# VectorE scales whole-precision heads' probabilities; products of constants beside nine heads; weight words raised to a least value; last rows in one block

## The chip, the cores and the metric

The kernel runs on one NeuronCore of a Trainium2 chip. The core has five engines that each work through a list of their own, in order: TensorE (PE; its weight loads are shown apart as PEld), VectorE (DVE), ScalarE (ACT), GpSimd (POOL) and SyncE (SP), which here only issues DMAs. TensorE writes its results to PSUM, which has eight banks; the others work in SBUF and, except GpSimd, in PSUM. The metric is the device time of one execution in microseconds (us), lower is better.

## The reference

Attention with a memory term over 8 batches and 8 heads, 576 rows of 64 each, and behind it a feed-forward network over all 4608 rows:

```python
def _attn_ref(q, k, v, M_prev, z_prev, beta):          # q, k, v: 8 x 8 x 576 x 64
    scores = scale * np.matmul(q, k.transpose(0, 1, 3, 2))
    scores = np.where(causal, -1e9, scores)
    a = np.exp(scores - scores.max(-1, keepdims=True))
    a /= a.sum(-1, keepdims=True) + 1e-09
    local = np.matmul(a, v)
    q_p = phi(q)                                        # elu(q) + 1
    mem_out = (q_p @ M_prev) / (q_p @ z_prev + 1e-6)
    g = 1 / (1 + np.exp(-beta))                         # one per head
    return g * mem_out + (1 - g) * local

def _moe_ref(x, w_in, w_out):                           # x: 4608 x 512, w_in: 512 x 2048
    h = x @ w_in
    return (h * (1 / (1 + np.exp(-h)))) @ w_out         # 4608 x 512
```

q, k, v and M_prev are float32; w_in and w_out come as float64, so the kernel gets them as pairs of 32-bit words.

## The kernel before

**Three streams.** `attention()` works on the 64 heads (batch, head) one after the other. In iteration n it advances `scores` of head n and `values` of head n-1 by turns, one `yield` of each at a step, ten steps to a head. `preparation()` turns the 32 chunks (128 x 512 words) of the weights into the form that the matmuls take; `ffn()` works on 18 units of 256 rows. The loop at the end of the function mixes them: about three chunks of weights to a head, and units from the moment on at which the eight heads of the first batch are done (`done[0] >= H`). This gives a program order; the scheduler of the framework makes from it a fixed list for each engine, which the engine then follows strictly in order, waiting at the head of the list for what an instruction needs.

**Scores of a head.** L221 transposes q and k (DVE). Then come rows in blocks of 128: for block i the matmul L250 writes 128 x 128(i+1) scores to a PSUM bank of `ps_s`, L252 (DVE) adds the mask and takes the minimum of the negated scores, L254 (ACT) takes the exponential and its sum. 576 is four and a half blocks. The last 64 rows are done as two halves of their columns, 256 and 320, one on partitions 0 to 63 and one on 64 to 127 of one tile: two matmuls (L271 for whole heads, L274 for the others), two reductions L284, and `halves_of` (L289 to L291), which joins the two halves' minima and later their sums by three small DVE instructions each time. L299 and L302 make one factor for each row from the sums and the gate, and five L304 (POOL) scale the five blocks of probabilities.

**Whole heads and split heads.** The first `N_WHOLE = 10` heads are "whole": their matmuls take float32 operands as they are, and each such matmul shows as two TensorE instructions. The other 54 heads split each operand into a rounded part and a rest (float32r), and each matmul is one instruction.

**Values of a head.** L351 transposes the memory term's rows, L376, L393 and L384 transpose the scaled probabilities (L393 and L384 those of the last rows, two halves at a time), ACT copies them (L401), L414 and L422 multiply them with M_prev and v, and L425 copies the result out.

**Weights.** For each chunk ACT scales the low words (L150), DVE shifts and joins the high words (L152, L154), POOL adds the low part (L156), ACT takes the magnitude of the high words (L158), DVE multiplies the result with "magnitude at least LEAST" (L159), ACT rounds (L161) and POOL takes the rest (L162).

**Feed-forward.** L552 makes h (128 x 256, in the one bank of `ps_h`), L563 to L569 make silu, L532 adds to the two accumulators `acc`, each one bank of `ps_a`.

## Time and profile before

| | |
|---|---|
| median of 3 runs | 1315.68 us (1314.75 to 1318.42) |
| the profiled execution's own time | 1315.66 us |
| its span, first to last instruction | 1313.9 us |
| busy: PE, PEld, DVE, ACT, POOL | 96%, 83%, 68%, 67%, 63% of the span |
| mean granted TensorE clock | 0.975 |

The profile has three parts, each with another limit. Up to about 175 us only whole heads and weight preparation run; from there to about 1110 us feed-forward units run beside the heads; then feed-forward units run alone. The page gives busy shares over the whole span, so a stage is read from the view by windows, and the order of events on an engine from its timeline. In a timeline row the columns are start and duration in us, engine, line, operation, output and inputs, the tile sizes (for a matmul: stationary, then moving), the number of merged instructions and, in brackets, the idle time ahead and what ended it. The granted clock is known only from the first change of it that the profiler recorded; earlier windows show 1.00.

### The profile page before, as it was taken

What the parts mean: (1) busy time and instruction counts of PE and PEld (TensorE: products, weight loads), DVE (VectorE), ACT (ScalarE), POOL (GpSimd) and SP (SyncE); (2) the same over time, 40 slices, a digit from 0 to 9 for tenths busy, and PEclk for the clock granted to TensorE, in tenths of its full rate; (3) what the DMA queues carried; (4) which work ended last, traced back from release to release, by engine and by line L of the source; (5) the groups of instructions that cost most, each with busy time, mean ns of one, the idle gap of its engine ahead of it and who ended that gap; (6) DMA issues with size and microseconds to landing.
All of it is one profiled execution on the core that took longest, in us unless ns stands there. A gap on an engine that the chain in (4) does not pass through costs nothing.

```text
span 1313.9 us, 24653 instructions
## 1 busy us (share of the span) xinstructions
PE 1266.3 (96%) x7858; PEld 1084.0 (83%) x7858; DVE 898.1 (68%) x2472; ACT 884.5 (67%) x2143; POOL 822.9 (63%) x1133
## 2 busy tenths in 40 slices
PE   6988999999999999999999999999999999999998
PEld 2343458888999989998988989899898998999997
DVE  7988875778777777787767777777877775332222
ACT  6777866777787777777777777787878774322222
POOL 6878995777777777777777777767767763000000
PEclk9987779999999999999999999999999999999999
DMA  6766555555455555555555555555545432444444
GB/s 165 188 184 168 162 134 164 144 131 146 125 145 147 138 153 138 150 131 149 137 137 143 145 138 154 137 137 136 158 129 156 123 123 81 145 154 149 152 156 143
DMA packets 302994, 190.39 MB, mean 145 GB/s; under 512 B 258832, under 2 KB 267024, under 8 KB 302864
## 3 DMA queue, kind: packets, MB, share of 16 engines
q1 hardware_dynamic: 302864, 188.82, 51.9%
q8 instruction: 62, 1.02, 0.3%
q14 instruction: 68, 0.56, 0.1%
HBM read 173.02 MB, written 15.73 MB: 144 GB/s over the span
## 4 chain that ended last, share of the span: by engine, by line
PE 73%; DVE 11%; ACT 6%; issue 3%; POOL 3%; DMA 3%; SPq 1%; POOLq 0%; DVEq 0%; ACTq 0%
PE h L552 28%; PE acc L532 25%; PE x L422 7%; PE s L250 5%; PE tp L376 4%; PE tq L351 1%; PE x L414 1%; DVE s L252 1%; DVE wy L159 1%; DVE pl L407 1%; DVE st L290 1%; ACT p L254 1%; POOL p L304 1%; PE s L274 1%; DVE wy L154 1%
## 5 line engine op out<-in xcount | busy, mean ns | idle before, releaser
L552 PE MATMUL h<-xu,wi 128*128 128x256 f32 x2592 | 376.8, 287 | 8.7 <-DVE th L564 6.1
L552 PEld LDWEIGHTS h<-xu,wi 128*128 128x128 f32 x2592 | 343.0, 191 | 24.6 <-DVE th L564 7.8
L532 PE MATMUL acc<-wo,g 128*128 128x512 f32 x864 | 243.0, 398 | 0.0
L532 PE MATMUL acc<-flow,g 128*128 128x512 f32 x864 | 231.0, 394 | 0.5 <-DMA flow<-wo_s 0.5
L304 POOL TENSOR_SCALAR p<-p,st 128x384 f32<-128x384 f32 (+3 forms) x320 | 182.8, 592 | 75.3 <-DVE st L302 72.2
L564 DVE SCALAR_TENSOR_TENSOR th<-th,h 128x512 f32<-128x512 f32 x144 | 98.2, 683 | 143.5 <-ACT th L563 141.7
L532 PEld LDWEIGHTS acc<-flow,g 128*128 128x128 f32 x864 | 158.8, 188 | 33.6 <-DMA flow<-wo_s 1.0
L254 ACT ACTIVATE p<-s,st 128x128 f32<-128x128 f32 (+3 forms) x256 | 134.9, 528 | 69.9 <-DVE st L252 52.8
L569 POOL TENSOR_TENSOR g<-th,g 128x512 fp32r<-128x512 f32 x108 | 140.2, 1298 | 48.7 <-ACT g L567 46.9
L532 PEld LDWEIGHTS acc<-wo,g 128*128 128x128 f32 x864 | 149.1, 189 | 18.9 <-POOL p L304 0.5
L563 ACT ACTIVATE th<-h 128x512 f32<-128x512 f32 x144 | 85.9, 597 | 99.7 <-PE h L552 97.4
L407 DVE TENSOR_TENSOR pl<-tp,ph 128x384 fp32r<-128x384 f32 x216 | 118.5, 551 | 34.6 <-ACT ph L406 31.3
L252 DVE CUSTOM_DVE_ANT_0 s<-s,mask 128x128 f32<-128x128 f32 (+3 forms) x256 | 125.3, 491 | 23.1 <-PE s L250 19.6
L567 ACT CAST g<-th 128x512 fp32r<-128x512 f32 x144 | 89.2, 620 | 53.0 <-DVE th L564 52.1
L376 PE MATMUL tp<-ident,p 128*128 128x128 f32 x640 | 121.8, 291 | 3.2 <-POOL p L304 2.5
L552 PE MATMUL h<-xu,flow 128*128 128x256 f32 x864 | 122.6, 283 | 0.0
L406 ACT CAST ph<-tp 128x384 fp32r<-128x384 f32 x216 | 104.7, 490 | 26.1 <-PE x L422 21.2
L552 PEld LDWEIGHTS h<-xu,flow 128*128 128x128 f32 x864 | 112.8, 191 | 1.9 <-issue 0.3
L376 PEld LDWEIGHTS tp<-ident,p 128*128 128x128 f32 x640 | 82.2, 148 | 28.6 <-POOL p L304 9.0
L422 PE MATMUL x<-pl,vs 128*128 128x256 f32 x324 | 82.1, 308 | 0.9 <-DVE pl L407 0.9
L232 POOL TENSOR_TENSOR kk<-tt,kk 64x576 fp32r<-64x576 f32 x54 | 77.4, 1432 | 5.0 <-ACT kk L230 1.2
L422 PE MATMUL x<-ph,vs 128*128 128x320 f32 (+4 forms) x378 | 78.2, 275 | 1.4 <-POOL vs L316 0.8
(104 smaller groups left out, 2409.5 us busy)
## 6 DMA issues: line engine op xcount, KB each, us to landing
flow<-wo_s SPq DMA_DIRECT2D x144, 512.0 KB, 3.6
flow<-wi_s SPq DMA_DIRECT2D x72, 512.0 KB, 3.8
raw<-in_k SPq DMA_DIRECT2D x128, 72.0 KB, 2.5
raw<-in_q SPq DMA_DIRECT2D x128, 72.0 KB, 2.7
out<-o SPq DMA_DIRECT2D x36, 256.0 KB, 4.2
wraw<-in_moe_w_in SPq DMA_DIRECT2D x16, 512.0 KB, 4.4
qn<-in_q SPq DMA_DIRECT2D x64, 128.0 KB, 2.9
vr<-in_v SPq DMA_DIRECT2D x64, 128.0 KB, 2.5
```

The lines of the kernel that those rows point to most:

```text
L252: anchor["dve"] = nc.vector.tensor_tensor_reduce(s, s, mask[:, 3 * P - P * i:], QS, 3.0e38, ALU.add, ALU.min, st[:, i:i + 1]).ins
L254: nc.scalar.activation(pt, s, AF.Exp, bias=st[:, i:i + 1], scale=-1.0, accum_out=st[:, 10 + i:11 + i])
L304: nc.gpsimd.tensor_scalar(pb[x], pb[x], st[:, 15 + x:16 + x], 1.0, op0=ALU.mult, op1=ALU.mult)
L376: nc.tensor.transpose(t[:, o:o + P], pb[i][:, P * j:P * j + P], ident)
L406: nc.scalar.copy(ph[:, 0:o], t[:, 0:o])
L407: nc.vector.tensor_tensor(out=pl[:, 0:cut], in0=t[:, 0:cut], in1=f(ph[:, 0:cut]), op=ALU.subtract)
L422: nc.tensor.matmul(x[0:rows, q0:n], vs[0:n_k, j], part[0:n_k, o:o + n - q0], start=False, stop=last)
L532: nc.tensor.matmul(acc[t], ta, tb, start=p == 0 and c == 0 and n == 0, stop=p == NP - 1 and c == 1 and n == len(terms) - 1)
L552: nc.tensor.matmul(h[:, c], ta, tb, start=kk == 0 and n == 0, stop=kk == KD - 1 and n == len(terms) - 1)
L564: nc.vector.scalar_tensor_tensor(out=th, in0=th, scalar=1.0, in1=h, op0=ALU.add, op1=ALU.mult)
L567: nc.scalar.copy(hi, th)
L569: late.tensor_tensor(out=lo, in0=th, in1=f(hi), op=ALU.subtract)
```

## The change

1. *Scaling.* For whole heads the five scalings of the probabilities go from GpSimd to VectorE. For the other heads they stay.
2. *Last rows in one block.* For whole heads the last 64 rows are one block on 64 partitions: two matmuls of 288 columns into the two banks of one `ps_a` tile `sw`, one reduction over 64 x 2 x 288, one exponential, and one small copy in place of the six small instructions. The probabilities go to a tile `pw` (64 x 576), which takes the one buffer of the tag `vs`; in `values` they are transposed block by block, five transposes in place of three.
3. *Accumulators.* `ps_a` has one buffer of two banks in place of two buffers of one bank; the two accumulators of a unit are the halves of one tile.
4. *Products of constants.* `keep_busy` issues two 128 x 128 float32 matmuls (stationary: the identity; moving: 128 columns of the mask that are zero) at each step of iterations 0 to 8, each ordered behind the attention's latest matmul. They write a tile `idle` in the bank of `ps_h`, which nothing reads. There are 176 of them.
5. *Weights.* The magnitude of the high words is taken first and raised to LEAST (now 2^-15, without the factor 1.125) by a VectorE instruction with one input, ahead of the shift; the last multiplication goes away. There are still three VectorE instructions to a chunk; two of them now have one input (before, one).

```diff
+WARM = 2
...
-    LEAST = 2.0 ** -15 * 1.125
+    LEAST = 2.0 ** -15
...
-    ps_a = ctx.enter_context(tc.tile_pool(name="ps_a", bufs=2, space=PSUM))
+    ps_a = ctx.enter_context(tc.tile_pool(name="ps_a", bufs=1, space=PSUM))
...
+            nc.scalar.activation(w, f(high), AF.Abs)
+            nc.vector.tensor_scalar(w, w, LEAST, None, op0=ALU.max)
             nc.vector.tensor_scalar(
-                y, high, 3, 0x3FFFFFF8, op0=ALU.logical_shift_left, op1=ALU.bitwise_and)
+                y, y, 3, 0x3FFFFFF8, op0=ALU.logical_shift_left, op1=ALU.bitwise_and)
             nc.vector.scalar_tensor_tensor(
                 out=y, in0=high, scalar=0xC0000000, in1=y, op0=ALU.bitwise_and, op1=ALU.bitwise_or)
             nc.gpsimd.tensor_tensor(out=y, in0=y, in1=low, op=ALU.add)
-            nc.scalar.activation(f(high), f(high), AF.Abs)
-            nc.vector.scalar_tensor_tensor(
-                out=w, in0=f(high), scalar=LEAST, in1=w, op0=ALU.is_ge, op1=ALU.mult)
...
+        if whole:
+            n2 = S // 2
+            pt = pool.tile([P, S], F32, tag="vs", name="pw", bufs=NB["vs"])
+            banks = ps_a.tile([P, T // P, DM], F32, tag="a", name="sw")
+            for x in range(2):
+                nc.tensor.matmul(
+                    banks[up, x, 0:n2], qq[0:64, S - LAST:S], tt[0:64, n2 * x:n2 * x + n2], start=True, stop=True)
+            yield
...
+            anchor["dve"] = nc.vector.tensor_tensor_reduce(
+                s, s, seen, QS, 3.0e38, ALU.add, ALU.min, st[up, i:i + 1]).ins
+            nc.scalar.activation(
+                pt[up].rearrange("p (a b) -> p a b", a=2), s, AF.Exp, bias=st[up, i:i + 1], scale=-1.0,
+                accum_out=st[up, 10 + i:11 + i])
+            pb.append(pt)
+            yield
+            nc.vector.tensor_copy(st[down, 10 + i:11 + i], st[up, 10 + i:11 + i])
...
         for x in range(NQ):
-            nc.gpsimd.tensor_scalar(
-                pb[x], pb[x], st[:, 15 + x:16 + x], 1.0, op0=ALU.mult, op1=ALU.mult)
+            rows = up if whole and x == i else slice(0, P)
+            (nc.vector if whole else nc.gpsimd).tensor_scalar(
+                pb[x][rows], pb[x][rows], st[rows, 15 + x:16 + x], 1.0, op0=ALU.mult, op1=ALU.mult)
...
+                    if whole:
+                        for j, x0, q0 in spans:
+                            at, n_k = x0 + n - q0, min(P, S - P * j)
+                            nc.tensor.transpose(
+                                t[0:n_k, at - LAST:at], last[0:LAST, P * j:P * j + n_k], ident[0:LAST, 0:LAST])
...
+    def keep_busy(behind):
+        for _ in range(WARM):
+            with tc.issue_after(behind):
+                nc.tensor.matmul(idle[:, 0:P], ident, mask[:, 0:P], start=True, stop=True)
...
+    idle = ps_h.tile([P, 2 * T], F32, tag="h", name="idle")
...
+                behind = anchor.get("pe")
                 for _ in range(FIRST_STEPS):
                     one = one and next(first, "end") != "end"
...
+                if behind and n <= H:
+                    keep_busy(behind)
...
-            bank, tag = (ps_s, "s") if done[0] == B * H and u % 2 else (ps_a, "a")
-            acc = [bank.tile([P, DM], F32, tag=tag, name="acc") for _ in range(T // P)]
+            if done[0] == B * H and u % 2:
+                acc = [ps_s.tile([P, DM], F32, tag="s", name="acc") for _ in range(T // P)]
+            else:
+                banks = ps_a.tile([P, T // P, DM], F32, tag="a", name="acc")
+                acc = [banks[:, t] for t in range(T // P)]
```

The scheduler makes new lists from this. TensorE's list before, at the boundary between two whole heads (the last products of one head's values, `x`, and the first transposes of the next one's probabilities, `tp` from the tiles p_963 to p_1041):

```order
L422 MATMUL x<-ph,vr 64x64
L351 MATMUL tq<-ident,e 128x128 x2
L351 MATMUL tq<-ident,e 64x128
L250 MATMUL s<-tt,qf 128x512
L422 MATMUL x<-ph,vr 64x320
L271 MATMUL s<-tt,qf 64x256
L271 MATMUL s<-tt,qf 64x320
L376 MATMUL tp<-ident,p_963 128x128
L414 MATMUL x<-qp,mr 64x256
L376 MATMUL tp<-ident,p_988 128x128 x2
```

The same place in the changed list (`idle` is the output of the products of constants, `sw` the last rows' scores; lines are those of the changed file):

```order
L461 MATMUL idle<-mask,ident 128x128 x2
L370 MATMUL tq<-ident,e 128x128 x2
L370 MATMUL tq<-ident,e 64x128
L270 MATMUL sw<-tt,qf 64x288 x2
L251 MATMUL s<-tt,qf 128x128
L251 MATMUL s<-tt,qf 128x256
L446 MATMUL x<-ph,vr 64x320
L461 MATMUL idle<-mask,ident 128x128 x8
L395 MATMUL tp<-ident,p_867 128x128
L395 MATMUL tp<-ident,p_881 128x128 x2
L461 MATMUL idle<-mask,ident 128x128 x4
```

Twelve of a head's twenty products stand at this boundary, around the first transposes of the next head; the other eight stand in pairs between its products with v. VectorE's changed list around the scaling of one whole head (`p_515` to `p_572` and `pw` are the five blocks of probabilities, `wy` a chunk of weights):

```order
L284 COPY st<-st 64x1
L317 SCALAR_TENSOR_TENSOR st<-st,over 128x5
L320 RECIPROCAL st<-st 128x5
L155 TENSOR_SCALAR wy<-wy 128x512
L323 TENSOR_SCALAR p_515<-p_515,st 128x128
L323 TENSOR_SCALAR p_540<-p_540,st 128x256
L323 TENSOR_SCALAR p_556<-p_556,st 128x384
L323 TENSOR_SCALAR p_572<-p_572,st 128x512
L323 TENSOR_SCALAR pw<-pw,st 64x576
L156 TENSOR_SCALAR wy<-wy 128x512
```

The five scalings now stand in VectorE's list directly behind the factors, with weight work ahead and behind; before, they stood in GpSimd's list. In TensorE's list the feed-forward matmuls of the first unit, of which a few (nine of 24) stood among heads 2 to 8, now all stand behind the last product of constants; from the tenth head on the number of feed-forward matmuls ahead of each head differs from before by some tens at most, and 1236 of them stand behind the last transpose in both lists.

More of the change, by code (lines that the diff above doesn't have):

```diff
@@ L261, in scores @@
         i = NQ - 1
-        pt = pool.tile([P, 3 * P], F32, tag=f"p{i}", name=f"p{i}", bufs=P_BUFS)
-        halves = []
-        for side, other, x0, x1, o in ((slice(0, LAST), slice(LAST, P), 0, SPLIT, P),
-                                       (slice(LAST, P), slice(0, LAST), SPLIT, S, 0)):
-            s = ps_s.tile([P, 512], F32, tag="s", name="s")
-            s = s[:, 0:x1 - x0]
-            row = pair[side, o:o + x1 - x0]
-            more = mask[side, 0:x1 - x0] if x1 < S else mask[side, 4 * P + x0 - x1:]
-            if whole:
-                nc.tensor.matmul(s[side], qq[0:64, S - LAST:S], tt[0:64, x0:x1], start=True, stop=True)
-            else:
+        up, down = slice(0, LAST), slice(LAST, P)
+        if whole:
[6 more added lines that the diff above has]
+            yield
+            s = banks[up, :, 0:n2]
+            seen = mask[up, 0:n2]
+            seen = bass.AP(seen.tensor, seen.offset, [list(seen.ap[0]), [3 * P + LAST - n2, 2], [1, n2]])
+            anchor["dve"] = nc.vector.tensor_tensor_reduce(
[7 more added lines that the diff above has]
+        else:
+            pt = pool.tile([P, 3 * P], F32, tag=f"p{i}", name=f"p{i}", bufs=P_BUFS)
+            halves = []
+            for side, other, x0, x1, o in ((slice(0, LAST), slice(LAST, P), 0, SPLIT, P),
+                                           (slice(LAST, P), slice(0, LAST), SPLIT, S, 0)):
+                s = ps_s.tile([P, 512], F32, tag="s", name="s")
+                s = s[:, 0:x1 - x0]
+                row = pair[side, o:o + x1 - x0]
                 q0 = S - LAST if side.start == 0 else S
@@ L421, in values @@
                         n_k = LAST if whole and j == NQ - 1 else P
-                        nc.tensor.matmul(
-                            x[0:rows, q0:n], vs[0:n_k, j], part[0:n_k, o:o + n - q0], start=False, stop=last)
+                        anchor["pe"] = nc.tensor.matmul(
+                            x[0:rows, q0:n], vs[0:n_k, j], part[0:n_k, o:o + n - q0], start=False, stop=last).ins
             if whole:
```

37 lines of the change are left out of this document (18 added, 19 removed).

## The prediction

> **What bounds the kernel now.** I read the windows first, since the page's busy shares are means over stages with different limits. Columns: stretch, its length, then busy us and instructions of PE, PEld, DVE, ACT and POOL, granted clock, DMA share, GB/s.
>
> ```profile
> PEclk9987779999999999999999999999999999999999
> 0.00:17.50 17.50, 6.12 (x11) 2.39 (x11) 10.08 (x33) 7.49 (x17) 12.23 (x32) 1.00 0.61 133
> 17.50:66.80 49.30, 46.26 (x100) 18.64 (x100) 44.24 (x107) 37.17 (x90) 40.49 (x37) 1.00 0.72 191
> 66.80:175.00 108.20, 93.54 (x288) 43.67 (x286) 95.52 (x213) 83.23 (x199) 94.66 (x85) 0.73 0.60 163
> 300.00:1110.00 810.00, 798.42 (x5422) 734.34 (x5422) 605.00 (x1786) 612.03 (x1516) 585.75 (x861) 1.00 0.51 139
> 1110.00:1313.90 203.90, 198.63 (x1265) 179.50 (x1263) 57.39 (x96) 56.30 (x105) 1.32 (x2) 1.00 0.45 148
> ```
>
> From 300 us on TensorE is busy for 98% of the time at the full clock: that part is as long as TensorE's list, and the list keeps its matmuls. So what the change is worth is decided ahead of it, in the stage of whole heads. There, from 17.5 to 175 us, PE and DVE are each busy for 139.8 of 157.5 us, POOL for 135.2, ACT for 120.4: four engines near their limit, none alone. The last row of the page's slices says where TensorE's clock was low. The timeline of TensorE says more, because the record starts late:
>
> ```profile
> 17.49 0.90 PE L351 MATMUL tq<-ident,e 128*128 128x128 f32 x3 [1.31 <-POOL e L334]
> 44.07 2.07 PE L250 MATMUL s<-tt,qf 64*128 64x512 f32 x2
> 63.48 3.44 PE L422 MATMUL x<-ph,vr 128*64 128x320 f32 x8
> 67.85 0.64 PE L271 MATMUL s<-tt,qf 64*64 64x256 f32 x2
> 68.42 0.50 PE L552 MATMUL h<-xu,wi 128*128 128x256 f32 x2
> 71.35 0.70 PE L250 MATMUL s<-tt,qf 64*128 64x256 f32 x2 [0.18 <-DVE st L284]
> 73.93 0.44 PE L376 MATMUL tp<-ident,p 128*128 128x128 f32 x2
> 74.21 0.27 PE L393 MATMUL tp<-ident,p 128*128 128x128 f32 x1
> 74.41 0.91 PE L250 MATMUL s<-tt,qf 64*128 64x384 f32 x2
> 75.25 0.44 PE L376 MATMUL tp<-ident,p 128*128 128x128 f32 x2
> 75.73 1.12 PE L250 MATMUL s<-tt,qf 64*128 64x512 f32 x2
> 76.78 0.75 PE L414 MATMUL x<-qp,mr 64*64 64x320 f32 x2
> 80.64 0.64 PE L271 MATMUL s<-tt,qf 64*64 64x256 f32 x2 [0.83 <-ACT p L254]
> 86.18 0.79 PE L250 MATMUL s<-tt,qf 64*128 64x128 f32 x2 [3.76 <-DVE st L284]
> 175.00 0.90 PE L351 MATMUL tq<-ident,e 128*128 128x128 f32 x3
> ```
>
> The same product of 512 columns took 2.07 us at 44 us and 1.12 us at 76 us, 1.85 times as long: before about 67 us the clock was half, whatever the 1.00 of the window says. From the first L351 (head 0, 17.49) to the ninth (head 8, 175.00) are eight heads: **19.7 us a head**. At the full clock a head's TensorE work fits between the L271 at 67.85 and the one at 80.64: 12.79 us, less the gaps of 0.83 and 0.18 and the two L552 (0.43 to the next start), is **11.35 us**. So a good third of TensorE's 17.5 busy us a head is the slow clock.
>
> What sets the clock? Two windows:
>
> ```profile
> 23.20:48.00 24.80, 24.80 (x52) 9.76 (x52) 24.16 (x54) 19.62 (x46) 19.96 (x18) 1.00 0.79 218
> 79.80:86.20 6.40, 1.42 (x6) 0.40 (x5) 6.24 (x16) 4.29 (x12) 5.17 (x7) 0.89 0.81 208
> ```
>
> For 24.8 us TensorE had no gap and stayed at half clock (the 2.07 us product lies in it); the clock rose right after 3.4 us of L422, whose stationary tile fills all 128 rows, where scores (64*128, 64*64) fill 64. It fell after the wait at the end of a head, 1.42 busy of 6.40 us. My reading: a few us of nearly unbroken work on all rows raise it, a window with little work drops it. The Trainium skill ("TensorE: Matmul & The Clock Gate", "Why this matters for your kernels") says that TensorE kept busy for 4 us on end gets the full clock; the 24.8 us disagree. By that rule the stage before would already have been at the full clock from about 27 us on, and the products could only cost.
>
> **The change part by part.** *Products of constants.* Twenty a head, 128 rows by 128 columns, float32, so two instructions each. No such product is in the trace. Lower bound: two transposes of that size start 0.28 us apart from what follows (73.93 to 74.21), 0.14 each, and a product is two such instructions: 0.28. Upper bound: a score product takes 0.84 us for 384 columns (74.41 to 75.25) and 1.05 for 512 (75.73 to 76.78), so 0.21 for 128 columns more and 0.42 for 128 in all. I take 0.30, near the transposes, which have the same stationary tile and stand in runs as the products do. That is 6.0 us a head (5.6 to 8.4). Two more transposes a head add 0.28. TensorE's head becomes 11.35 + 0.28 + 6.0 = 17.6 us if the clock is held. I think it is: twelve of the twenty stand at the end of a head, where the falls began, and fill 3.6 us; TensorE's moving tile in a transpose is the identity, nearly all zeros, so zeros are no reason that they don't count.
>
> The other engines, from the groups between 17.5 and 175 us (nine sets of rows):
>
> ```profile
> L154 DVE SCALAR_TENSOR_TENSOR wy<-wraw,wy 128x512 uint32<-128x512 uint32 x29 | 28.6, 987 | 0.5
> L159 DVE SCALAR_TENSOR_TENSOR wy<-wraw,wy 128x512 f32<-128x512 f32 x30 | 28.3, 952 | 0.3 <-POOL wy L156 0.2
> L152 DVE TENSOR_SCALAR wy<-wraw 128x512 uint32<-128x512 uint32 x29 | 20.1, 695 | 0.2
> L290 DVE TENSOR_TENSOR st<-st 64x1 f32<-64x1 f32 x18 | 8.4, 466 | 0.2
> L252 DVE CUSTOM_DVE_ANT_0 s<-s,mask 128x512 f32<-128x512 f32 x9 | 6.2, 685 | 0.1
> L284 DVE CUSTOM_DVE_ANT_0 pair<-s,mask 64x320 f32<-64x320 f32 x9 | 4.4, 494 | 7.2 <-PE s L271 7.1
> L284 DVE CUSTOM_DVE_ANT_0 pair<-s,mask 64x256 f32<-64x256 f32 x9 | 3.6, 404 | 2.4 <-PE s L271 2.4
> L284 DVE DVE_READ_ACCUMULATOR2_ANT st<- 64x1 f32 x18 | 1.4, 76 | 0.0
> L291 DVE COPY st<-st 64x1 f32<-64x1 f32 x18 | 2.7, 147 | 0.6
> L304 POOL TENSOR_SCALAR p<-p,st 128x384 f32<-128x384 f32 x18 | 13.6, 754 | 0.0
> L304 POOL TENSOR_SCALAR p<-p,st 128x256 f32<-128x256 f32 x9 | 8.0, 887 | 0.0
> L304 POOL TENSOR_SCALAR p<-p,st 128x128 f32<-128x128 f32 x9 | 7.3, 811 | 3.1 <-DVE st L302 2.8 <-DVE nrm L333 0.3
> L304 POOL TENSOR_SCALAR p<-p,st 128x512 f32<-128x512 f32 x9 | 7.1, 788 | 0.0
> ```
>
> *Last rows.* Off DVE go the L284 (4.4 + 3.6 + 1.4 = 9.4 us, 1.04 a head) and the six small ones (8.4 + 2.7, and 2.7 again for L289, a copy of the same form: 13.8, 1.53 a head). On come one reduction over 576 columns, 0.685 x 576/512 + 0.08 = 0.85, and a copy, 0.15. Net -1.6 us a head.
>
> *Scaling.* POOL loses 36.0 us in nine sets, 4.0 a head of its 16.9. DVE gains five instructions with one SBUF input. How long such an instruction is alone, and how far it is stretched, show the durations by line (min, median, max in ns):
>
> ```profile
> L121 DVE TENSOR_SCALAR ql<-ident x8: 224/232/245, 4.0 to 5.4; 64x128 fp32r<-64x128 f32 x8
> L152 DVE TENSOR_SCALAR wy<-wraw x32: 379/427/1517, 8.3 to 182.4; 128x512 uint32<-128x512 uint32 x32
> L290 DVE TENSOR_TENSOR st<-st x128: 106/229/1279, 21.5 to 1096.7; 64x1 f32<-64x1 f32 x128
> ```
>
> 0.23 us for 128 columns and 0.38 for 512 give 0.23, 0.28, 0.33, 0.38 and 0.41 for the five, 1.63 in all; stretched as L152 is in this stage (0.695 against 0.379) 3.2. I take 2.7, nearer the upper end, since weight work still runs on POOL. The stretch itself is plain in L290: a sum of two columns that takes 0.106 us alone took up to 1.279. The Trainium skill ("SBUF — State Buffer", "Who interferes with whom") gives the reason: VectorE and GpSimd share a pair of ports, and a scaling from SBUF to SBUF on VectorE takes it and blocks the other engine wholly. L290's row agrees, and the rule speaks against moving work between just these two; POOL, with 4.0 us less, has room for 2.7 us of blocking.
>
> *Weights.* 29 chunks in eight heads are 3.6 a head. Two of three instructions now have one input: 0.695 + 0.695 + 0.987 = 2.38 against 2.63 us, -0.9 a head; if the stretch shrinks with POOL's load, up to -1.8. I take -1.3.
>
> DVE's head: 17.5 - 1.6 + 2.7 - 1.3 = **17.3 us** (15.8 to 18.2 from the bounds). Its idle time was 17.7 us, 2.2 a head, of which the L284 rows alone show 9.5 waiting for products at a slow clock; at the full clock I halve it: 18.4 a head. TensorE: 17.6, and 0.9 for waits on DVE in an in-order list, 18.5; and a lost clock now and then (3.4 us at half clock cost 1.6 of work, in one head of eight): **18.7 us a head**.
>
> *The rest at nothing.* The products of head 0 lie in TensorE's 11.4 idle us before 17.5. The accumulators' common tile waits for both copies of a unit instead of one each, but two h of 24 matmuls stand between; without that cover it would cost one more copy of a bank a unit, some 0.7 us by the L252 row of 512 columns, 12 us for 18 units. The feed-forward matmuls that stood ahead of head 8 are nine, at 0.2 us each (68.42 to 68.85 for two) under 2 us, and TensorE does them later instead of a wait.
>
> **The sum.** Eight heads at 19.7 - 18.7 = 1.0 us: -8.0. Between the ninth L351 and the feed-forward run stand six more products: +1.8. Against the profiled execution's 1315.66 us (the median of the runs is 1315.68) that gives **1309.5 us**.
>
> **The rivals.** *A. More relief.* DVE at its lower bound, products at 0.28: TensorE's 17.2 plus half a us of waits, 17.7 a head, -16 + 1.7: 1301 us. For it speaks that POOL has 4 us less to collide with; against, that DVE has five more instructions that collide. *B. The products are dear.* At 0.42 TensorE's head is 11.6 + 8.4 + 0.9 = 20.9: +9.6 + 2.5, 1328 us, slower. It decides from a price of 0.36 on, where the head is 19.7 again. For it: TensorE has no free time in the changed list. Against: runs of equal stationary tiles are the transposes' case. *C. The clock isn't held*, because waits outlast the products or products with zeros don't count: at half clock a head is 1.85 x 17.6 = 32.6 us; half of the time so, 25 a head, +42 + 3: 1360 us. It turns the gain round from 7% of the time on. For it: the clock fell within 6.4 us with four fifths idle. *D. DVE stays the limit*, 18.2 plus 1.5: 19.7, nothing gained: 1317 us. For it: DVE was idle for only a ninth of the stage. *The change doesn't do what it says* is a part of C.
>
> **Chances.** The forecast 0.48, A 0.12, B 0.13, C 0.12, D 0.15. What a measurement here can tell from no change is about 0.3%, 4 us. The forecast's own range, 1301 to 1315, lies four fifths below 1311.7; with A that is faster 0.50; D and the rest of the forecast make same 0.22; B, C and a tail of D slower 0.28. The range that holds 8 in 10 leaves out most of C and the end of A: 1298 to 1327.
>
> **What would show it.** The L370 of head 8 near 167 us instead of 175 and the feed-forward part after it unchanged in length. The clock at 1.00 from about 20 us on and the 512-column product near 1.1 us throughout; runs of eight products of 2.3 to 2.6 us (3.4 would be B). DVE's scalings at 0.3 to 0.7 us each, POOL near 13 us a head. TensorE's waits before the transposes small; if they are long and the clock low behind them, it is C. A longer stretch after head 8 would mean that I was wrong about the accumulators.

## The result and the profile after

The changed kernel takes 1331.51 us (median of 4 runs, 1327.44 to 1336.87) against 1315.22 us (median of 4) for the kernel before: a ratio of 1.0121 (95% interval 1.0077 to 1.0165), so **1.2% slower** where 1309.5 us was forecast. The profiled execution took 1327.44 us with a span of 1325.7; the differences below are between the two profiled spans, 1313.9 and 1325.7, 11.8 us apart. The profiled execution is the shortest of the four; the others took 1329.1, 1333.9 and 1336.9 us with mean granted clocks of 0.989, 0.984 and 0.982 instead of 0.990. So the profiles show 11.8 of the 16.3 us between the medians, and no trace shows where the rest lies.

Four marks cut the execution: the first transposes of head 0 and of head 8 (L351 before, L370 after), and the end of the first unit (unit 0) and of the fourteenth (unit 13, after which no head is left), taken as the start of the timeline row with ScalarE's last copy out of a unit's accumulators. Where that row holds both of a unit's copies, the mark is up to 0.8 us earlier than the last copy itself; from copy to copy the later stage is 12.8 us longer instead of the 13.6 below. Windows between these marks, the kernel before (columns as in the prediction's first fence):

```profile
17.49:175.00 157.51, 139.81 (x386) 62.33 (x386) 139.76 (x320) 120.41 (x288) 135.16 (x121) 0.81 0.64 172
175.00:254.10 79.10, 79.10 (x484) 65.13 (x483) 50.98 (x141) 53.26 (x135) 57.82 (x76) 0.97 0.56 152
254.10:1132.60 878.50, 864.22 (x5862) 794.00 (x5860) 649.28 (x1906) 655.22 (x1621) 617.71 (x907) 1.00 0.51 138
```

and the changed kernel:

```profile
21.15:170.44 149.29, 142.34 (x701) 85.17 (x700) 142.83 (x288) 116.47 (x281) 103.36 (x81) 0.93 0.68 184
170.44:252.20 81.76, 80.69 (x501) 65.63 (x500) 50.66 (x140) 51.55 (x130) 45.87 (x62) 1.00 0.52 138
252.20:1144.30 892.10, 868.87 (x5873) 797.19 (x5872) 648.41 (x1909) 654.32 (x1624) 618.18 (x910) 1.00 0.50 136
```

Head 0 starts 3.7 us later, the eight heads take 8.2 us less, the way from head 8 to the end of unit 0 takes 2.7 us more, and the stage of units beside heads **13.6 us more**; behind it nothing changes (181.3 and 181.4 us). 3.7 - 8.2 + 2.7 + 13.6 = 11.8. The last row is the surprise: TensorE has nearly the same work there (5862 and 5873 instructions recorded), but 23.2 us without any (892.10 less 868.87) instead of 14.3, and 4.7 us more of busy time.

The eight heads took the time that was forecast: 149.29 / 8 = 18.66 us a head (predicted 18.7), with the clock at 0.93 instead of 0.81. The timeline of TensorE in the changed kernel:

```profile
17.63 3.68 PE L461 MATMUL idle<-mask,ident 128*128 128x128 f32 x20
21.15 0.49 PE L370 MATMUL tq<-ident,e 128*128 128x128 f32 x3
...
30.77 1.12 PE L251 MATMUL s<-tt,qf 64*128 64x512 f32 x2
...
39.94 2.05 PE L461 MATMUL idle<-mask,ident 128*128 128x128 f32 x16
```

The product of 512 columns takes 1.12 us at 31 us: full clock, where the kernel before had half until 67. It didn't stay full:

```profile
54.30:67.90 13.60, 13.60 (x39) 7.84 (x40) 13.50 (x28) 9.88 (x25) 7.90 (x7) 0.50 0.53 137
95.20:102.10 6.90, 6.90 (x20) 3.47 (x20) 6.80 (x14) 6.78 (x17) 6.72 (x6) 0.51 0.63 166
```

Eight products of constants at full clock take 2.05 us. But the ten in the first row stand ahead of head 0's first transposes and hold them back. VectorE in the eight heads of the changed kernel, by groups (busy us, mean ns, then idle time and its releasers):

```profile
L159 DVE SCALAR_TENSOR_TENSOR wy<-wraw,wy 128x512 uint32<-128x512 uint32 x29 | 30.0, 1042 | 0.2
L156 DVE TENSOR_SCALAR wy<-wy 128x512 uint32<-128x512 uint32 x29 | 21.3, 739 | 0.2
L323 DVE TENSOR_SCALAR p<-p,st 128x128 f32<-128x128 f32 (+3 forms) x32 | 20.9, 712 | 0.2
L155 DVE TENSOR_SCALAR wy<-wy 128x512 f32<-128x512 f32 x29 | 19.4, 670 | 0.6 <-ACT wy L154 0.6
L277 DVE CUSTOM_DVE_ANT_1 sw<-sw,mask 64x576 f32<-64x576 f32 x8 | 6.1, 758 | 0.0
L323 DVE TENSOR_SCALAR pw<-pw,st 64x576 f32<-64x576 f32 x8 | 4.0, 503 | 0.0
L284 DVE COPY st<-st 64x1 f32<-64x1 f32 x8 | 1.2, 148 | 0.4
L277 DVE DVE_READ_ACCUMULATOR2_ANT st<- 64x1 f32 x8 | 1.0, 131 | 0.0
```

The scalings cost (20.9 + 4.0) / 8 = 3.1 us a head, the weights 70.7 us for 29 chunks where the three lines took 77.0 before, the last rows' reduction, its read-out and the copy 8.3 us for eight heads.

In the later stage, these are TensorE's longest waits before (254 to 1132 us; us in total, times, longest):

```profile
PE h L552 <- DVE th L564: 6.1, 11, 1.0
PE s L250 <- ACT p L254: 4.0, 7, 0.8
```

and in the changed kernel (252 to 1144 us):

```profile
PE h L590 <- DVE th L602: 11.2, 17, 1.3
PE s L251 <- ACT p L255: 3.3, 4, 1.4
PE x L438 <- DVE xt L454: 2.5, 2, 2.2
PE s L251 <- DVE st L303: 1.7, 2, 1.0
```

No row names the copies out of the accumulators: no instruction waits longer for the common tile. What differs is which work stands beside which. A place where both lists have the same rows shows how a wait grows, before:

```profile
328.24 0.44 PE L250 MATMUL s<-kk,qq 128*128 128x384 f32 x1 [0.43 <-ACT p L254]
328.52 0.34 PE L250 MATMUL s<-kk,ql 128*128 128x384 f32 x1
329.26 1.66 PE L552 MATMUL h<-xu,wi 128*128 128x256 f32 x12 [0.40 <-DVE th L564]
```

and after:

```profile
328.42 0.44 PE L251 MATMUL s<-kk,qq 128*128 128x384 f32 x1 [0.56 <-ACT p L255]
328.70 0.34 PE L251 MATMUL s<-kk,ql 128*128 128x384 f32 x1
329.99 2.28 PE L590 MATMUL h<-xu,wi 128*128 128x256 f32 x12 [0.95 <-DVE th L602]
```

The wait for the silu is 0.55 us longer, and the twelve matmuls behind it take 2.28 us instead of 1.66: the clock dropped for a moment (0.91 in the mean from 320 to 340 us). A lost clock raises the busy time, but this is a rare case. At 532.67 us a longer wait is followed by the same twelve matmuls at full speed:

```profile
532.67 1.67 PE L590 MATMUL h<-xu,wi 128*128 128x256 f32 x12 [1.35 <-DVE th L602]
```

The mean clock of the whole stage is 1.00, so most of the 4.7 us of busy time isn't explained by the clock.

### The profile page after: what moved, and what is told of

It reads as the page before. It is cut to its first block, busy times and chain, and to the rows that moved or that the text cites. A ratio compares the mean times of both kernels' runs of the same rounds, so it can differ in the third digit from the quotient of the medians.

```text
span 1325.7 us, 25267 instructions
## 1 busy us (share of the span) xinstructions
PE 1282.4 (97%) x8230; PEld 1116.5 (84%) x8230; DVE 901.4 (68%) x2452; ACT 880.5 (66%) x2143; POOL 780.3 (59%) x1083
## 4 chain that ended last, share of the span: by engine, by line
PE 70%; DVE 12%; ACT 7%; issue 4%; POOL 4%; DMA 2%; SPq 1%; DVEq 0%; POOLq 0%; ACTq 0%
PE h L590 26%; PE acc L570 24%; PE x L446 6%; PE s L251 4%; PE tp L395 3%; DVE s L253 1%; PE x L438 1%; DVE th L602 1%; PE tq L370 1%; PE idle L461 1%; DVE pl L431 1%; DVE p L323 1%; ACT p L255 1%; POOL r L347 1%; DVE tt L222 1%
## 5 line engine op out<-in xcount | busy, mean ns | idle before, releaser
L590 PE MATMUL h<-xu,wi 128*128 128x256 f32 x2592 | 370.2, 286 | 12.3 <-DVE th L602 12.3
L590 PEld LDWEIGHTS h<-xu,wi 128*128 128x128 f32 x2592 | 340.6, 190 | 26.8 <-DVE th L602 11.2
L323 POOL TENSOR_SCALAR p<-p,st 128x128 f32<-128x128 f32 x270 | 142.6, 547 | 89.0 <-DVE st L320 88.8
L570 PEld LDWEIGHTS acc<-wo,g 128*128 128x128 f32 x864 | 148.8, 188 | 20.9 <-issue 1.0
L590 PE MATMUL h<-xu,flow 128*128 128x256 f32 x864 | 127.3, 286 | 0.0
L395 PE MATMUL tp<-ident,p 128*128 128x128 f32 x640 | 113.3, 275 | 1.3 <-DVE pl L431 0.9
L395 PEld LDWEIGHTS tp<-ident,p 128*128 128x128 f32 x640 | 78.5, 140 | 18.5 <-DVE pl L431 1.7
L347 POOL TENSOR_TENSOR r<-e,zb 128x320 f32<-128x320 f32 x64 | 61.1, 955 | 41.0 <-DVE e L346 35.7
L236 POOL TENSOR_TENSOR ql<-tt,qq 64x512 fp32r<-64x512 f32 x54 | 70.2, 1300 | 23.7 <-ACT qq L232 18.3
```

Of the source, the lines that this page charges most:

```text
L323: (nc.vector if whole else nc.gpsimd).tensor_scalar(pb[x][rows], pb[x][rows], st[rows, 15 + x:16 + x], 1.0, op0=ALU.mult, op1=ALU.mult)
L395: nc.tensor.transpose(t[:, o:o + P], pb[i][:, P * j:P * j + P], ident)
L570: nc.tensor.matmul(acc[t], ta, tb, start=p == 0 and c == 0 and n == 0, stop=p == NP - 1 and c == 1 and n == len(terms) - 1)
L590: nc.tensor.matmul(h[:, c], ta, tb, start=kk == 0 and n == 0, stop=kk == KD - 1 and n == len(terms) - 1)
```

## The experiments

Line numbers below are of each kernel's own file. Ratios are to the kernel before, timed on the same chip, with 95% intervals.

**The edits apart.** Four kernels: the common tile alone (e1); scalings, weight words and products without the block of last rows and the common tile (e2); the changed kernel without products (e3); the products alone (e4).

```diff
# e1, against the kernel before
-    ps_a = ctx.enter_context(tc.tile_pool(name="ps_a", bufs=2, space=PSUM))
+    ps_a = ctx.enter_context(tc.tile_pool(name="ps_a", bufs=1, space=PSUM))
...
+                banks = ps_a.tile([P, T // P, DM], F32, tag="a", name="acc")
+                acc = [banks[:, t] for t in range(T // P)]
# e2 and e4, against the kernel before (e2 with the scalings and weight words too)
+                if behind and n <= H:
+                    keep_busy(behind)
# e3, against the changed kernel
-                if behind and n <= H:
-                    keep_busy(behind)
```

> The kernel before with one edit: the two accumulators of a unit are halves of one two-bank tile (edit 3 alone). Numbers to compare: from head 8's first transposed memory term (L351) to the end the kernel before takes 1138.9 us, the changed one 1155.3. Theory P (the common tile makes the list of the feed-forward part worse): this part is 1148 to 1158 us here, the stage ahead stays at 175 us, the total is 1324 to 1333. Theory H (the products of constants, which hold the bank of h until head 8, shift the feed-forward stream): no change here, 1315. Theory L (any edit deals the list of that part anew, better or worse): anywhere from 1305 to 1330.

> The changed kernel with its last rows in halves and its accumulators in two tiles, as before (edits 2 and 3 undone; scaling on VectorE, weights and products stay). Its feed-forward matmuls stand, from the third unit on, at the same places among the heads as before. Theory P: the part from head 8 on is 1139 to 1142 us, and with a first stage of about 171 to 174 us the total is 1310 to 1315. Theory H: that part is still 1150 or more, the total 1323 or more. Theory L: as P here, since the list is the one of before.

> The changed kernel without the products of constants (edit 4 undone), so the bank of h is free from the start; the accumulators keep their common tile. Theory P: the part from head 8 on stays at 1148 to 1158 us; the first stage without products at a slow clock 165 to 178 us. Theory H: that part falls to 1139 to 1143 us, the total to 1310 to 1318. Theory L: another list than the changed one's, 1140 to 1160. Is the clock the products' doing, it is at half here until about 65 us as before, and TensorE's 512-column product takes 2.0 us there.

> The kernel before with the products of constants alone (edit 4). Theory P: the part from head 8 on 1139 to 1142 us. Theory H: 1150 or more. For the first stage: VectorE and GpSimd keep their load (17.5 and 16.9 us a head), the clock is full from about 20 us on; if the clock was what held the heads, head 8 comes at 167 to 173 us, if the two other engines were, at 174 to 182.

Measured: e1 1319.15 us (1.0024, 1.0003 to 1.0046), e2 1320.51 (1.0049, 1.0026 to 1.0071), e3 1340.75 (1.0178, 1.015 to 1.0206), e4 1316.27 (1.0003, 0.9989 to 1.0016). The later stage took 883.1, 878.9, 897.7 and 877.6 us: longer with the common tile, about as before without it. No theory has all its numbers: P's for e1 (1324 us or more) and for e2 (1315 or less) failed, and e3's stage is long without the products, which speaks against H. The products do hold the clock: from 40 to 200 us it is 0.94 in the changed kernel and 0.73 without them (e3), 0.97 with them alone (e4) and 0.80 before. They bring head 8 forward by 6.2 us alone (168.8) and by 10.7 in the changed kernel (170.4 against 181.1 in e3), but in e4 the end of unit 0 came no earlier (255.9 against 254.1). There, head 8 met engines that weren't ready. VectorE and then TensorE in e4:

```profile
183.21 0.78 DVE L222 STREAM_TRANSPOSE tt<-raw 128x576 f32<-128x576 f32 x1 [3.52 <-DMA raw<-in_q]
```

```profile
PE h L564 <- DVE th L576: 2.6, 1, 2.6
```

The gain to head 8 was given back within two heads to a load of q and k, and to the silu queued behind it on VectorE.

**The first stage and the list.** The scalings alone (e5), the weight words alone (e6), and the pace of the units against the heads changed without any change of an operation, with two tiles (e7) and with the common tile (e8).

```diff
# e5, against the kernel before
-            nc.gpsimd.tensor_scalar(
+            (nc.vector if whole else nc.gpsimd).tensor_scalar(
# e6, against the kernel before (and the other lines of the weight words)
-    LEAST = 2.0 ** -15 * 1.125
+    LEAST = 2.0 ** -15
...
+            nc.scalar.activation(w, f(high), AF.Abs)
+            nc.vector.tensor_scalar(w, w, LEAST, None, op0=ALU.max)
# e7, against the kernel before; e8, against e1
-FFN_RATE = 0.22
+FFN_RATE = 0.225
```

> The kernel before with one edit alone: the whole-precision heads' five scalings a head run on VectorE instead of GpSimd. With products, the pair of scalings and weight words reached head 8 at 172.9 us where the products alone reached it at 168.8, so the pair costs some 4 us there. Theory S (the scalings cost it: some 2.7 us of VectorE work a head come back less than GpSimd's relief): head 8's first transpose 3 to 5 us later than the 175.0 us before, the time 1318 to 1320 us. Theory W (the weight words cost it): head 8 within 1 us of 175.0, the time 1315 to 1316. Theory of the prediction (GpSimd's relief outweighs VectorE's work where TensorE is not the limit): head 8 at 173 to 175.

> The kernel before with one edit alone: the weight words raised to a least value (a maximum of one operand in place of the compare-and-multiply, another order of the steps). Theory W (the weight words cost the 4 us of the first stage, by the other order on VectorE, where the maximum waits for ScalarE's absolute value): head 8's first transpose at 178 to 180 us, the time 1318 to 1320. Theory S (the scalings cost it): head 8 within 1 us of 175.0, or up to 3 us earlier, since the edit takes work from VectorE; the time 1313 to 1316.

> The kernel before, accumulators in two tiles, with the constant that paces the feed-forward part against the heads at 0.225 in place of 0.22: no operation changes, only the order in which heads and feed-forward steps stand in the lists (from unit 2 on, 3 to 15 of the next unit's matmuls stand ahead of a unit's last accumulations, where before 8 to 22 did). Theory P (the common tile of the accumulators costs the time): the stretch from the end of unit 0 to the end of unit 13 stays within 2 us of the 878.5 us before. Theory L (each other list costs by itself; the list before is a good draw): this stretch grows by 3 to 15 us, the time 1318 to 1330.

> The same pace 0.225 with the accumulators in one common tile, all else as before. Theory P: the stretch from unit 0 to unit 13 is again 4 to 5 us longer than that of the kernel with two tiles and the same pace, as it was at 0.22 (883.1 against 878.5). Theory L: the difference to the kernel with two tiles takes another value, between -5 and +10 us, with the list: here 8 to 15 matmuls of the next unit stand ahead of a unit's last accumulations, against 3 to 15 with two tiles.

Measured: e5 1326.05 us (1.0091, 1.006 to 1.0121), head 8 at 185.7; e6 1319.06 (1.0029, 1.0013 to 1.0045), head 8 at 168.3; e7 1340.21 (1.0191, 1.0162 to 1.022); e8 1327.47 (1.0096, 1.0067 to 1.0125).

Theory S holds, and by more than expected: alone, the scalings cost 10.7 us to head 8 and 17.1 to the end of unit 0 in the profiled execution. That one took 1331.65 us, 5.6 above e5's median, so the median execution must have lost nearer 12 us (an estimate, from the medians' difference of 11.6 and a later stage as before). VectorE's and GpSimd's groups in e5 (20 to 175 us) say how:

```profile
L304 DVE TENSOR_SCALAR p<-p,st 128x384 f32<-128x384 f32 (+3 forms) x40 | 24.8, 684 | 0.1
```

```profile
L156 POOL TENSOR_TENSOR wy<-wy,wraw 128x512 uint32<-128x512 uint32 x26 | 37.3, 1446 | 21.9 <-DVE wy L154 17.6 <-issue 1.3 <-ACT p L254 0.8
```

In the kernel before the same line (17.5 to 175 us) had been:

```profile
L156 POOL TENSOR_TENSOR wy<-wy,wraw 128x512 uint32<-128x512 uint32 x30 | 44.6, 1488 | 10.7 <-DVE wy L154 2.9 <-DVE st L299 2.4 <-ACT xt L425 2.2
```

GpSimd was relieved of the scalings and used the time to wait for VectorE, 17.6 us on one line instead of 2.9. The weight words (e6) brought head 8 forward by 6.7 us, more than the 3 that theory S allowed.

Theory P, by which the common tile costs the time, falls. With two tiles and the other pace the later stage took 904.7 us, 26 more than before; with the common tile and that pace 887.8, so here the common tile is 17 us *better*. e7's stage by the window, and its longest wait:

```profile
251.80:1156.50 904.70, 876.24 (x5854) 803.34 (x5853) 656.61 (x1904) 652.70 (x1622) 619.88 (x909) 0.99 0.48 134
```

```profile
PE tp L376 <- DVE qp L359: 12.1, 7, 2.4
```

In the changed kernel this wait is 0.2 us in all: each list has its own. Theory L is left, that the length is that of the list; its ranges were too narrow for both (26 us more where 3 to 15 was expected, and -17 for the tile where -5 to 10 was).

**One edit undone, and two edits alone.** e9 leaves the scalings on GpSimd and keeps the rest of the change. e10 has the weight words and the products alone, these without the last iteration.

```diff
# e9, against the changed kernel
-            (nc.vector if whole else nc.gpsimd).tensor_scalar(
+            nc.gpsimd.tensor_scalar(
# e10, against e6 (and the rest of keep_busy)
+                if behind and n <= H - 1:
```

> The changed kernel with one edit undone: the five scalings a head of whole-precision heads stay on GpSimd; weight words, products, last rows in one block and the common tile stay. Theory S (the scalings on VectorE alone cost the first stage some 10 us): head 8's first transpose at 158 to 162 us against 170.4 in the changed kernel, that is 10.7 us earlier. Theory L (same list, same length): its TensorE list from unit 0 on goes as that of the kernel with the common tile alone, so the stretch from the end of unit 0 to the end of unit 13 is 883.1 us within 1.5, as there, not 892.1 as in the changed kernel. With 79 to 87 us from head 8 to the end of unit 0 the time is 1304 to 1314 us. Rival (the other edits leave nothing once the scalings are gone, because another engine holds head 8): head 8 at 167 to 171, the time above 1320.

> Two of the edits alone, chosen by the runs so far: the weight words (head 8 6.7 us earlier by themselves) and the products, these beside the first eight steps of heads instead of nine; scalings on GpSimd, last rows in two halves, accumulators in two tiles. Its TensorE list agrees with that of the kernel before from unit 2 on. Theory L: the units 2 to 13 last as long as before to 0.3 us each, the stretch from unit 0 to unit 13 878 us within 2. Theory A (the two gains to head 8 add up): head 8 at 162 to 164 us. Theory H (the products beside the ninth step gave the 8 us back between head 8 and the end of unit 0): without them 79 to 81 us from head 8 to the end of unit 0, the time 1302 to 1306; if H is wrong 85 to 88 us there and 1309 to 1312.

Measured: e9 1326.46 us (1.0066, 1.0037 to 1.0095); e10 1316.17 (0.9997, 0.9982 to 1.0012). On the later stage both expectations held: 882.7 us for e9 (883.1 in e1, whose list it shares from unit 2 on) and 877.6 for e10. On the first stage the additions failed. e9's head 8 came at 180.9 us, not 158 to 162: in the profiles, undoing the edit that alone costs 10.7 us made it 10.4 us *later* (how much of that is the execution and not the kernel, see below). e10's head 8 came at 164.1 as added up, but unit 0 ended at 255.3: now a feed-forward matmul at head 8 waited 4.14 us for its input from VectorE, and the clock fell behind it:

```profile
165.40 0.38 PE L563 MATMUL h<-xu,wi 128*128 128x256 f32 x1
169.92 3.36 PE L563 MATMUL h<-xu,wi 128*128 128x256 f32 x14 [4.14 <-DVE xu L516]
173.20 2.07 PE L250 MATMUL s<-tt,qf 64*128 64x512 f32 x2
```

So H, as put for e10, is wrong too: it isn't the products beside the ninth step that give the gain back. In e4 and e10 TensorE, early at head 8, found the feed-forward's inputs not yet made. That isn't so for every early head 8: e6, there at 168.3, kept 4.3 of its 6.7 us (unit 0 ended at 249.8).

**The same list with and without the edits.** e11 has the scalings, the weight words, the products (not beside the first step) and the block of last rows, but the accumulators in two tiles and so the block's reduction in two parts, arranged so that its list agrees with that of the kernel before; e12 is the changed kernel with fewer products and the changed kernel's list.

```diff
# e11, against the changed kernel (and ps_a with bufs=2, acc as in the kernel before)
-            banks = ps_a.tile([P, T // P, DM], F32, tag="a", name="sw")
+            sw = [ps_a.tile([P, DM], F32, tag="a", name="sw")[up, 0:n2] for _ in range(2)]
...
# e11 and e12
-                if behind and n <= H:
+                if behind and 1 <= n <= H:
```

> All five edits' operations, but with the accumulators in two tiles again (the block of last rows takes the two tiles one after the other: two reductions and two exponentials, their minima and sums joined on VectorE), and products from the second step of heads on, not beside the first. Built so that its TensorE list agrees with that of the kernel before in 13 of 14 units, where the changed kernel's agrees in none. Theory L (the rest of the kernel lasts as long as its list says, whatever the edits): units 1 to 13 as before to 0.3 us each, 878.5 within 2 from the end of unit 0 to that of unit 13, against 892.1 in the changed kernel. With the end of unit 0 at 250 to 257 the time is 1305 to 1314 us, near what was predicted. Theory P (the edits themselves, by the products, the words or the block, slow the later stage): 885 us or more there, the time 1318 or more.

> The changed kernel with one thing taken away: the products beside the first step of heads (a run of ten products that held head 0's first transpose back by some 3.7 us). Its list from unit 0 on is word for word that of the changed kernel. Theory L: 892.1 us within 1.5 from the end of unit 0 to that of unit 13, units as in the changed kernel to 0.3 us each. Head 0's first transpose at 16 to 18 us. If that delay is passed on to the end, the end of unit 0 comes 3 to 4 us earlier (248 to 249) and the time is 1323 to 1325; if the later heads take it up, 1327 to 1328.

Measured: e11 1323.43 us (1.0073, 1.0057 to 1.0088); e12 1342.35 (1.0217, 1.0194 to 1.0241). The later stage of e11:

```profile
262.20:1140.60 878.40, 864.29 (x5870) 794.55 (x5869) 648.46 (x1910) 656.52 (x1623) 619.88 (x910) 1.00 0.50 138
```

878.4 us against 878.5 before, and TensorE's busy time to 0.1 us the same: with the list of before, the edits other than the common tile cost nothing there. The common tile e11 leaves out. But e9 has it, as the changed kernel does, and with e1's list takes 882.7 us, so at least 9.4 of the 13.6 us are the list's; the other 4.2 are those of the tile together with the list it brings, which no run separates. The lengths of the units, from one end to the next, and what the lists share (tile numbers and lines left out):

| kernel | units 1 to 13, us | TensorE's list |
|---|---|---|
| before | 72.1 65.0 70.0 66.1 67.0 69.2 66.8 67.5 66.6 69.2 67.9 66.8 64.3 | |
| e11 | 72.2 65.1 69.9 66.1 67.0 69.1 66.9 67.6 66.6 69.2 67.8 66.8 64.2 | as before from the end of unit 1 |
| e5 | 71.9 64.4 69.9 66.1 67.1 69.2 66.8 67.5 66.6 69.2 67.8 66.8 65.0 | as before from the end of unit 2 |
| e6 | 70.8 70.7 69.3 68.5 68.6 69.2 66.8 67.5 66.6 69.2 67.9 66.8 64.2 | other, as before from the end of unit 5 |
| e1 | 70.7 70.4 70.3 68.0 67.5 66.9 67.3 67.5 67.4 67.0 67.4 68.1 64.8 | another |
| after | 73.3 68.5 70.7 65.2 66.5 73.6 69.5 69.2 68.7 66.5 67.5 68.1 64.9 | a third |
| e12 | 74.5 68.5 72.3 65.1 66.5 73.6 71.0 69.2 68.7 66.5 67.5 68.1 64.8 | as after from the end of unit 0 |

e6 pays 8 us in the units where its list is another, and less than 0.2 us a unit of difference is left where it is the same. (e5's last unit is 0.7 us longer by the mark alone: its two copies have a row each.) With after's list e12 repeats ten units to 0.1 us; three are 1.2 to 1.6 us longer (896.3 in all, 892.1 within 1.5 expected).

The first stage again failed to follow: unit 0 ended at 262.2 in e11 (250 to 257 expected) and at 270.1 in e12 (248 to 249), 18 us later than in the changed kernel, for ten products taken from the head of the list. e12's profiled execution, 1348.96 us, is again 6.6 above its median.

**The early clock.** In e11 and e12 a product of constants between 20 and 40 us took 0.24 and 0.28 us per instruction, in the changed kernel 0.16. e13 moves e11's products from the second iteration to the first; e14 and e15 do it with last rows in halves, e14 with the scalings, weight words and products, e15 with the weight words and products.

```diff
# e13, against e11; e15, against e10 (there n <= H - 1)
-                if behind and 1 <= n <= H:
+                if behind and n <= H and n != 1:
# e14, against e2 (there n <= H)
+                if behind and n < 7 and n != 1:
```

> The kernel with all edits and two tiles, with the products of the second step of heads moved to the first step (first, and third to ninth). The list from unit 1 on is as before, so 878.4 within 1 from the end of unit 0 to that of unit 13. Theory W (the products beside head 0 bring TensorE to full clock at 20 us, and that is what the changed kernel's first stage has over the kernels that came late): mean of a product between 20 and 40 us at 0.15 to 0.18 us (0.24 without them), the end of unit 0 at 250 to 255 instead of 262.2, the time 1309 to 1315. Theory D (the first stage hangs on where TensorE's clock falls later on, and an early start at full clock decides little): the end of unit 0 at 258 to 268, the time 1318 to 1328.

> Scalings on VectorE, weight words and products (first step, third to seventh), last rows in two halves, two tiles; list from unit 1 on as before. Theory W: product mean between 20 and 40 us 0.15 to 0.18, the end of unit 0 at 250 to 255, the time 1309 to 1314. Theory D: the same kind of kernel with products beside all nine steps ended unit 0 at 258.8; 256 to 265 here, the time 1316 to 1324.

> Weight words and products (first step, third to ninth), scalings on GpSimd, last rows in two halves, two tiles; list from unit 2 on as before. Theory W: product mean between 20 and 40 us 0.15 to 0.18, the end of unit 0 at 246 to 252 (the weight words alone ended it at 249.8), the time 1303 to 1310, faster than the kernel before. Theory D: 253 to 262, the time 1314 to 1323.

Measured: e13 1324.32 us (1.0064, 1.0041 to 1.0088), unit 0 at 261.1; e14 1321.50 (1.0039, 1.0021 to 1.0057), unit 0 at 260.1; e15 1313.47 (0.9984, 0.9973 to 0.9996), unit 0 at 252.5. The later stage took 878.6, 879.2 and 877.6 us. Theory W, that the full clock at 20 us is what the changed kernel has over the others, isn't decided by these three. e13's ten product instructions between 20 and 40 us (0.14 us each, as expected) are the end of the run that stands ahead of head 0, which ends at 21.4; the clock then fell again, and the product of 512 columns took as long as without:

```profile
20.00:40.00 20.00, 18.95 (x67) 8.95 (x66) 15.35 (x44) 15.94 (x41) 7.89 (x7) 0.74 0.87 234
30.72 2.02 PE L251 MATMUL s<-tt,qf 64*128 64x512 f32 x2
```

In e14 and e15 no product stands between 20 and 40 us, and the clock there is 0.66 and 0.60. Theory D's ranges held for e13 and e14; e15's end of unit 0 lies between the two theories'. What speaks against W is e9: it has the changed kernel's products, its product of 512 columns takes 1.12 us at 31 us as well, and its unit 0 ended at 263.3. The early clock isn't enough; whether it is needed stays open.

Four kernels that carry the products and the block differ in the clock further on, here from 40 to 200 us in the changed kernel, e13, e11 and e9, one fence each:

```profile
40.00:200.00 160.00, 153.85 (x785) 96.46 (x785) 145.17 (x298) 120.57 (x292) 108.16 (x91) 0.94 0.63 172
```

```profile
40.00:200.00 160.00, 150.80 (x723) 90.89 (x722) 146.36 (x321) 117.51 (x294) 108.86 (x85) 0.89 0.58 163
```

```profile
40.00:200.00 160.00, 154.04 (x729) 93.47 (x727) 141.54 (x320) 117.04 (x291) 110.13 (x86) 0.87 0.58 163
```

```profile
40.00:200.00 160.00, 151.61 (x736) 94.02 (x735) 125.91 (x240) 114.01 (x276) 127.38 (x124) 0.87 0.57 160
```

Against 0.94 they lose 8.0, 11.2 and 11.2 us of full-speed time (0.05 and 0.07 of 160), and end unit 0 8.9, 10.0 and 11.1 us later than the changed kernel. TensorE is busy for 94 to 96% of this stretch in these four, so a lost clock is lost time there. The account doesn't carry over to e2, whose last rows are in halves: its clock is 0.96, TensorE is busy for 89%, and unit 0 ended at 258.8.

Why the clock fell in one and not in the other stays open, and part of it isn't the kernel: executions of one kernel differ as much. The ten executions of e13 took from 1316.9 us at a mean clock of 0.988 to 1329.1 at 0.976, the five of e9 from 1320.6 at 0.990 to 1328.3 at 0.983, and the four of the changed kernel from 1327.4 at 0.990 to 1336.9 at 0.982. (Not all kernels follow it: e11 took 1322.9 us at 0.993 and 1323.4 at 0.979.) The profiled execution is the longest of e9's and the shortest of the changed kernel's. At a clock of 0.990 in both, e9 is 6.8 us shorter, while its later stage is 9.4 shorter: by this estimate its first stage is some 3 us longer than that of the changed kernel, not the 11.1 of the profiles. So one trace of each kernel doesn't tell differences of some 10 us in the first stage. The later stage isn't so uncertain, since nine profiles with the same list agree to 1.6 us.

e15 is the one kernel whose whole interval lies ahead of the kernel before, by 0.16%, less than the 0.3% set as the smallest difference to be told here.

## Why the prediction was wrong, step by step

**The step that failed** is "the rest at nothing", with its premise that the part from 300 us on "is as long as TensorE's list, and the list keeps its matmuls". The list kept its matmuls and changed their order, and the order sets the waits, 14.3 or 23.2 us. The view on which it rested (98% busy at full clock) was read as a bound; the 2% were the part that the change could double. The front part even shows that the scheduler deals a new list; I priced a wait for the common tile, which doesn't appear, and not the new list. The profiled execution came 17.9 us above the forecast (1327.4 against 1309.5; the median 22.0), and 13.6 of them are this step, 3.7 the next one and 0.9 the way from head 8 to unit 0's end. What the other 4 us of the median are isn't shown. The sign I had named, a longer stretch after head 8, came true, with the list as the cause of most of it (9.4 to 13.6 us) and no wait for the accumulators.

**Products beside head 0 "lie in TensorE's 11.4 idle us"**: wrong, +3.7 us. The idle time was there, but the run of ten stands directly ahead of the first transposes, when the idle time is over.

**Price of a product**: somewhat below the bounds. 2.05 us for eight is 0.26 each at full clock (0.30 taken, 0.28 to 0.42 the bounds).

**Last rows**: right. 6.1 and 1.0 us for the reduction and its read-out and 1.2 for the copy, 1.04 us a head, against 2.57 in the forecast's rows: -1.5 (-1.6 forecast). **Scalings**: 3.1 us a head, at the upper bound of 3.2 instead of 2.7. **Weights**: -0.8 us a head ((77.0 - 70.7) / 8) instead of -1.3; the rows didn't shrink with GpSimd's load, 1042 ns against 987. Together VectorE's head is 17.9 us, not 17.3. **GpSimd**: 103.4 / 8 = 12.9 (13 forecast).

**18.7 us a head**: 18.66, in part by luck. TensorE was busy for 142.3 / 8 = 17.8 us a head (17.6 forecast) and idle for 0.9 (0.9). But the 17.6 was meant at full clock, with 0.2 more for slow clock. Twenty products at 0.26 are 5.1 us instead of 6.0, and a clock of 0.93 over 149.29 us stands for 10.5 us at full speed, 1.3 a head: two errors of nearly the same size and of opposite sign. VectorE's terms for scalings and weights were 0.9 us too small as well; its idle time, 0.8 us a head, was near the 1.1 taken.

**The sum by edits** describes the total and not how the edits act: in the profiles the scalings alone cost 17.1 us to the end of unit 0, the weight words gain 4.3 and the products cost 1.8; the three together (e2) come to +4.7 where the sum is +14.6. From the medians, less the differences of the later stage, it is about +5 against about +10 (an estimate). With executions of e5 and of e2 that lie up to 9 us apart, this isn't more than a sign.

**"Six more products, +1.8"** between head 8 and the run of feed-forward: +2.7 measured. The products there took 1.76 us (14 instructions recorded), as priced; TensorE was idle for 1.1 us besides (81.76 less 80.69), where it had no idle time before. In e4 and e10, earlier at head 8, the same stretch is 8.0 and 12.1 us longer than before: TensorE was idle for 5.1 and 5.0 us of it, and in e10 the clock was 0.91 instead of 0.97.

**The clock**: full by 31 us as forecast, but not held: 0.93 in the mean of the eight heads, with half clock from 54.3 to 67.9 and from 95.2 to 102.1 us, 20.5 of 149.29, twice the 7% of the time from which rival C would have turned the gain round at 0.30 a product. So C, given 0.12, came true in part, and kernels that differ in an edit or two lose 8 to 11 us more to it. The rule of the Trainium skill ("TensorE: Matmul & The Clock Gate", "Why this matters for your kernels") that I set aside, full clock after 4 us of unbroken work, stays contradicted: in e12 TensorE was busy for all of the 20 us from 20 to 40 us, and its products took 0.28 us per instruction there, twice the 0.14 that e13 shows.

**The scalings against the shared ports**: I had read the Trainium skill ("SBUF — State Buffer", "Who interferes with whom"), by which a scaling on VectorE can block GpSimd, as speaking against the move, and let GpSimd's spare 4 us pay for it. In e5 the move did cost, but the 17.6 us are a wait for VectorE's results, not for a port. Two of VectorE's weight rows became shorter (952 to 790 and 695 to 535 ns) where GpSimd was busy for 57% of the eight heads instead of 86%; that agrees with the Trainium skill, and the third, 987 and 981 ns, doesn't show it.

## What to carry to other kernels

Where a scheduler makes the lists, an edit can change the order far from its own place, and a stage that is "bound" at 98% can lose as much by it as the edit gains: compare the lists first, and judge an edit with the rest of the list held the same (eight kernels with other edits, and the list of the kernel before from the end of unit 2 on at the latest, took 877.6 to 879.2 us from the end of unit 0 to that of unit 13). Don't count a gain at the moment when one engine gets ahead, but at the next point where all of them must meet; in e10 head 8 came 10.9 us early and unit 0 ended 1.2 us late. Where executions of one kernel differ by 10 us, as in the first stage here, one trace each doesn't show whether edits add up: set the profiled execution against the others of its kernel first.

## What the runs showed of the hardware beyond what was expected

A short wait can cost more than itself, but needn't. Behind waits of 0.97, 0.56 and 0.95 us within 5 us the changed kernel's clock fell, and twelve matmuls took 2.28 us instead of 1.66; behind a single wait of 1.35 us the same twelve took 1.67. And two of VectorE's three weight instructions became faster when GpSimd had less to do: 952 to 790 ns and 695 to 535 in e5, while the small sums and minima of the last rows became slower (466 to 617 ns).
